# Channel attention on one core: the last loads, the packing of the last block and the re-read ring are rearranged

## The chip, the cores and the metric

The kernel runs on one core of one Trainium2 chip. Its time is the device time of one execution in microseconds (us); the figure for the kernel before is the median of three runs, 727.28 us (724.67 to 727.91). Stage times are read from one profiled execution of it.

## The reference

The input x has 384 x 384 pixels of 384 channels in bf16; w1 is 384 x 96 and w2 96 x 384.

```python
xf = x.reshape(B, H * W, C)
gap = jnp.mean(xf, 1)
gmp = jnp.amax(xf, 1)
h_a = gap @ w1
h_a = h_a * (h_a > 0)
h_m = gmp @ w1
h_m = h_m * (h_m > 0)
scale = _sigmoid(h_a @ w2 + h_m @ w2)
return x * scale[:, None, None, :]
```

Each channel's mean and maximum over all pixels go through a small two-layer gate, and every pixel is multiplied by the 384 gate values. All of x has to be read before the first product can be made.

## The kernel before, in words

The pixels are cut into 1152 "rows". One row is 128 pixels, one to a partition, with 384 channels each: 96 KB. The input and the output are 1152 rows each, and the core's SBUF holds only a part of them, so the kernel has two phases.

**First phase.** SP issues the loads (L396) in the order of the list `steps`. For each load TensorE adds the rows up with a vector of ones (L290; for the last four loads L306, straight into `gsum_ps`), and VectorE takes the maximum of the rows into the accumulator `acc` of 11 rows (L360). `acc` is worked on in two halves by turns. FEWER says at which load, counted from the end, it is folded from 11 rows to 8.

Some rows remain on the chip for the second phase, so they need not be read again. Eight blocks of 32 rows are packed into the space of 24 each: ScalarE tests that the high bytes are in a small range (`test`, L319 and L320), TensorE makes 16-bit words of them in PSUM (`pack`, L340, into `words_ps`, with weights of which two lie in `held`), and ScalarE takes the result (L346 and L347). Ten rows go to PSUM early (`kept_ps`, `kept_b`). 64 rows "stay" where transient rows lay before. Eight "late" rows are loaded into `d_places[0]` and transposed by TensorE into the PSUM bank of the words (`turn_over`, L366), eight "kept" rows into `d_places[1]`, and five "held" rows into `held`. `held` is also where the tests write their bytes and where two of the packing weights lie, so the held load, which is the last of all, can only be issued when the last test and the last words are done.

All other rows pass through and are read once more in the second phase.

**The gap.** After the last load SP issues, in this order: eight rows for the place that the last packing frees (L425), w1 (L426), w2 (L427), eight rows for `d_places[0]` as soon as the late rows have been transposed out of it (L439), and the eleven rows of the accumulator's own pixels in four pieces, as folding frees them (L437). TensorE's program in this stretch is: the turn of the sums (L301), the sums of the last four loads with the transposes of the late rows after the first of them (L306, L366, L306), then the first layer of the gate for the mean, which needs w1 (L430), then the transposes of the folded maximum (L450), the first layer for the maximum (L454) and the second layer (L456). An engine works off its program in order, so L450 can't start before L430 has. ScalarE makes the sigmoid (L457) and the second phase begins.

**Second phase.** VectorE multiplies rows by the gate (L462) and ScalarE's queue issues their stores (L471, L477, L512): first what stayed, then the ring. PLACES lists the places of the ring: a place is read again (L547, on SP) when the product of the rows that lay there has been stored, and its turn comes in order. TURNS says in which turn a packed block is unpacked by VectorE and ScalarE (L490, L495, L509); two finished blocks let the ring grow from 72 rows to 96 and to 120.

The order on every engine is the order in which the code records it (`manual_schedule`). DMAs get one of eight completion semaphores in turn, and a DMA waits until the one eight before it has landed.

These are the lists that set the end of the first phase. LAST_BLOCK's two loads, PASSING's eight, STAYING's ten and LAST_HELD's four are the last 24 loads; PACK_LAST puts the two halves of the last block's packing ahead of the 19th and the 11th load from the end.

```python
FEWER = {16: 8}
LAST_BLOCK = (10, 22)
PACK_LAST = {19: 0, 11: 1}
PASSING = ((0, 20), (20, 16), (36, 17), (53, 11), (0, 11), (11, 8), (19, 8), (27, 12))
REFILLS = (5, 6)
STAYING = ((39, (4, 8, 5, 8)), (0, (8, 4, 9, 8, 6, 4)))
LAST_HELD = ((8,), (4, 4), (5,))
```

Of the kernel before, what the change touches and what calls it, by code (L numbers as in the profile page):

```python
# [19 lines left out]
E4 = mybir.dt.float8e4  # L20
E3 = mybir.dt.float8e3
# [10 lines left out]
G = 8  # L32
PACKED = 8
# [14 lines left out]
LATE_ROWS = 8  # L48
BANK_ROWS = 2
RING_BYTES = 128  # L50
HELD_ROWS = 5
A = 11

FEWER = {16: 8}

ACC_PIECES = ((6, 11), (0, 6))

# [8 lines left out]
PACK_BEHIND = (0, 2, 1, 1, 0, 0, 1)  # L66

LAST_BLOCK = (10, 22)
PACK_LAST = {19: 0, 11: 1}
PASSING = ((0, 20), (20, 16), (36, 17), (53, 11), (0, 11), (11, 8), (19, 8), (27, 12))  # L70

REFILLS = (5, 6)
STAYING = ((39, (4, 8, 5, 8)), (0, (8, 4, 9, 8, 6, 4)))
LAST_HELD = ((8,), (4, 4), (5,))


PLACES = (
    ((0, 18), (18, 18), (36, 18), (54, 18)) * 3 + ((0, 24), (24, 24), (48, 24), (72, 24))
    + ((0, 30), (30, 30), (60, 30), (90, 30)) * 3 + ((0, 30), (30, 30), (60, 30), (90, 12))
)  # L80
FIRST_READ = (6, 12)
# [24 lines left out]
def kernel(  # L106
# [7 lines left out]
    nc = tc.nc  # L114
    P = nc.NUM_PARTITIONS
    B_, H, W_, C = x.shape
# [19 lines left out]
    at = 0  # L136

    def take(n):
        nonlocal at
        at += n  # L140
        return at - n, n

    for_psum = PSUM_ROWS + BANK_ROWS
    first_block = take(for_psum + A)
    packed_block = take(GP * PACKED)
    late_block, kept_block, held_block = (take(sum(pieces)) for pieces in LAST_HELD)
    stay = take(STAY_ROWS)
    refills = [take(PASSING[k][1]) for k in REFILLS]
    passing_at, n_pass = at, TOT - at
    between = [[take(n) for _, n in group] for group in BETWEEN]  # L150
    passing = [refills[REFILLS.index(k)] if k in REFILLS else take(n) for k, (_, n) in enumerate(PASSING)]
    assert at == TOT and sum(n for _, n in PLACES) == n_pass and held_block[1] == HELD_ROWS
    assert late_block[1] == LATE_ROWS and kept_block[1] == G and [n for _, n in refills] == [LATE_ROWS, G]
    assert sum(sum(p) for _, p in STAYING) == STAY_ROWS
    at = passing_at
    again = [take(n) for _, n in PLACES]
# [3 lines left out]
    ones_bf = small[:, 0:1]  # L160
# [6 lines left out]
    total = small[:, 1:2]  # L167
# [10 lines left out]
    acc = consts.tile([P, A, C], BF16)  # L178
# [3 lines left out]
    rows = nc.alloc_sbuf_tensor_at("rows", [P, HELD_ROWS + BODY_ROWS, C], BF16, offset=RING_BYTES).ap()  # L182
    held, body = rows[:, 0:HELD_ROWS, :], rows[:, HELD_ROWS:HELD_ROWS + BODY_ROWS, :]
# [3 lines left out]
    d_places = fourth[0:2]  # L187
# [12 lines left out]
    late = words_ps[:, 0:LATE_ROWS, :]  # L200
# [30 lines left out]
    weights = []  # L231
# [9 lines left out]
    def load(block, buf, pieces, lo=0):  # L241
        j = 0
        for m in pieces:
            steps.append(("load", block, buf[:, j:j + m, :], lo + j, lo + j + m))
            j += m
# [17 lines left out]
                steps.append(("pack", i, 1))  # L263
    i = PACKED - 1
    load(packed_block, body[:, D_AT[i]:, :], LAST_BLOCK, FOURTH_AT[i])
    steps += [("test", i, 0), ("test", i, 1), ("test", i, 2), ("judge",)]
    for k, b in enumerate(passing):
        fill(b, PASSING[k][0])
    for lo, pieces in STAYING:
        load(stay, body[:, lo:, :], pieces, lo)  # L270
    for block, buf, pieces in zip((late_block, kept_block, held_block), (*d_places, held), LAST_HELD):
        load(block, buf, pieces)

    loads = [st for st in steps if st[0] == "load"]
    tail_rows = sum(st[4] - st[3] for st in loads[len(loads) - SUM_TAIL:])
# [1 line left out]
    def high(rows, dt):  # L277
        return rows.rearrange("p n c -> p (n c)").bitcast(dt)[:, 1::2]
# [4 lines left out]
    def part(i, r):  # L283
        return homes[i][:, r * G:(r + 1) * G, :] if r < 3 else fourth[i]
# [39 lines left out]
    def test(i, what):  # L324

        if what == 2:
            test_one(high(part(i, 3), I8), 5 * i + 4)
            return
        n = G * C // 2
        a_b = homes[i][:, 0:2 * G, :].rearrange("p (r n) c -> p r (n c)", r=2).bitcast(I8)  # L330
        test_one(a_b[:, :, 2 * n * what + 1:2 * n * (what + 1):2], 5 * i + 2 * what)
        test_one(high(part(i, 2), I8)[:, n * what:n * (what + 1)], 5 * i + 2 * what + 1)

    def pack(i, half):
        n = G * C // 2
        span = slice(half * n, (half + 1) * n)
        for c in range(0, n, BANK):
            for r in range(4):
                for k, dt in enumerate((E4, E3)):
                    nc.tensor.matmul(  # L340
                        words[:, c:c + BANK], lhsT=weights[2 * r + k],
                        rhs=high(part(i, r), dt)[:, half * n + c:half * n + c + BANK],
                        start=(r == 0 and k == 0), stop=(r == 3 and k == 1),
                    )
        for r in (0, 1):
            nc.scalar.copy(out=high(part(i, r), U8)[:, span], in_=low(part(i, r + 2), U8)[:, span])  # L346
        nc.scalar.activation(  # L347
            out=part(i, 2).rearrange("p n c -> p (n c)").bitcast(U16)[:, span], in_=words,
            func=ACT.Copy, bias=32767.5,
        )  # L350

    def judge():
# [3 lines left out]
    def judged():  # L356
        nc.tensor.matmul(bad_ps, lhsT=total, rhs=ones_bf, start=True, stop=True)

    def maximum(out_, in0, in1):
        nc.vector.tensor_tensor(out=out_, in0=in0, in1=in1, op=ALU.max)  # L360
# [1 line left out]
    def turn_over(out_, rows):  # L362

        for r in range(LATE_ROWS):
            for q in range(CQ):
                nc.tensor.transpose(  # L366
                    out=out_[:, r, q * P:(q + 1) * P], in_=rows[:, r, q * P:(q + 1) * P], identity=ident_bf
                )
# [11 lines left out]
    for st in steps:  # L380
        if st[0] == "test":
            test(*st[1:])
        elif st[0] == "pack":
            pack(*st[1:])
        elif st[0] == "judge":
            judge()
        if st[0] != "load":
            continue
        _, block, rows, lo, hi = st
        m = hi - lo  # L390
        if len(loads) - nth in PACK_LAST:
            half = PACK_LAST[len(loads) - nth]
            if half == 1:
                judged()
            pack(PACKED - 1, half)
        nc.sync.dma_start(out=rows, in_=rows_of(xr, block)[:, lo:hi, :])  # L396
        if nth < len(loads) - SUM_TAIL:
            sums(rows, m, done, TOT - tail_rows)
# [12 lines left out]
        while j < m:  # L411
            c, e = halves[turn % len(halves)]
            turn += 1
            e = min(e, c + m - j)
            maximum(acc[:, c:e, :], acc[:, c:e, :], rows[:, j:j + e - c, :])
            j += e - c
        if block == late_block:
            turn_over(late, rows)
        elif block == first_block:
            nc.vector.tensor_copy(out=kept_ps.bitcast(U32), in_=rows[:, 0:PSUM_ROWS, :].bitcast(U32))  # L420
            nc.vector.tensor_copy(out=kept_b.bitcast(U32), in_=rows[:, PSUM_ROWS:for_psum, :].bitcast(U32))
        nth += 1


    nc.sync.dma_start(out=fourth[PACKED - 1], in_=rows_of(xr, refills[1]))  # L425
    nc.sync.dma_start(out=w1_sb, in_=w1.rearrange("(q p) m -> p q m", p=P))  # L426
    nc.sync.dma_start(out=w2_sb, in_=w2)  # L427
    nc.scalar.mul(out=gT[:, :, 0], in_=gsum_ps, mul=1.0 / HW)
# [1 line left out]
        nc.tensor.matmul(hTa_ps, lhsT=w1_sb[:, q, :], rhs=gT[:, q, 0:1], start=(q == 0), stop=(q == CQ - 1))  # L430
    nc.scalar.activation(out=hid_a, in_=hTa_ps, func=ACT.Relu)

    def acc_rows(ap, lo, hi):
        return rows_of(ap, first_block)[:, for_psum + lo:for_psum + hi, :]

    def load_acc(lo, hi):
        nc.sync.dma_start(out=acc[:, lo:hi, :], in_=acc_rows(xr, lo, hi))  # L437

    nc.sync.dma_start(out=d_places[0], in_=rows_of(xr, refills[0]))  # L439
    load_acc(folds[-1], A)  # L440
    half = folds[-1] // 2
    fold(half)
    load_acc(half, 2 * half)
# [111 lines left out]

    put_stay(*OPENING)
    put_acc()
    put(held_block, held, (HELD_ROWS,))
    put(kept_block, d_places[1], (G,))
    put(refills[0], d_places[0], (LATE_ROWS,))  # L560
    put_stay(*FIRST_PLACE)
# [75 lines left out]
```

## Time and profile before

| | |
|---|---|
| median of three runs | 727.28 us (724.67 to 727.91) |
| the profiled execution, its own time | 724.8 us |
| its span in the profile | 723.0 us |
| busy: VectorE, ScalarE, TensorE matmuls | 574.5, 358.8, 191.6 us |
| read from HBM, written to it | 192.14 MB, 113.25 MB |
| mean rate of the DMA engines | 423 GB/s |
| granted TensorE clock, mean | 0.627 |
| end of the last maximum of the first phase | 272.1 us |
| first product | 276.75 us |

The profile's page cuts the span into 40 slices of 18.1 us. Its DMA row gives the busy share of the 16 DMA engines in tenths and its GB/s row what they moved. The answer by windows gives the same for stretches that one names. The timeline has one line per group of instructions: start, duration, engine, line, operation, and in square brackets how long the engine was idle before it and who ended that. SPq and ACTq are the queues of SyncE and ScalarE on which DMAs are issued; the duration on such a line is that of the issue alone. A list of DMA issues gives KB and the time from issue to landing. The chain of waits is followed back from the last instruction of a stretch to what released it.

### The profile page before, as it was taken

What the parts mean: (1) busy time and instruction counts of PE and PEld (TensorE: products, weight loads), DVE (VectorE), ACT (ScalarE), POOL (GpSimd) and SP (SyncE); (2) the same over time, 40 slices, a digit from 0 to 9 for tenths busy, and PEclk for the clock granted to TensorE, in tenths of its full rate; (3) what the DMA queues carried; (4) which work ended last, traced back from release to release, by engine and by line L of the source; (5) the groups of instructions that cost most, each with busy time, mean ns of one, the idle gap of its engine ahead of it and who ended that gap; (6) DMA issues with size and microseconds to landing.
All of it is one profiled execution on the core that took longest, in us unless ns stands there. A gap on an engine that the chain in (4) does not pass through costs nothing.

```text
span 723.0 us, 4062 instructions
## 1 busy us (share of the span) xinstructions
PE 191.6 (26%) x1405; PEld 75.5 (10%) x1405; DVE 574.5 (79%) x463; ACT 358.8 (50%) x284; POOL 0.7 (0%) x6
## 2 busy tenths in 40 slices
PE   5667575966776681000000000000000000001000
PEld 2222222321322240000000000000000000001000
DVE  5699899999999998887876659837899999837300
ACT  6967969694989940350540635404544745000000
POOL 0000000000000000000000000000000000000000
PEclk9887987895978776555555555555555555555555
DMA  9999999999999999999999999999999999999997
GB/s 381 435 434 433 421 432 429 428 427 430 428 421 428 414 382 347 406 424 429 430 429 431 433 434 435 429 437 433 430 428 432 433 438 428 428 432 433 450 424 334
DMA packets 22422, 305.66 MB, mean 423 GB/s; under 512 B 2848, under 2 KB 3072, under 8 KB 8704
## 3 DMA queue, kind: packets, MB, share of 16 engines
q1 hardware_dynamic: 14336, 192.14, 62.6%
q10 hardware_dynamic: 8064, 113.25, 36.7%
q8 instruction: 11, 0.18, 0.1%
q14 instruction: 11, 0.09, 0.0%
HBM read 192.14 MB, written 113.25 MB: 422 GB/s over the span
## 4 chain that ended last, share of the span: by engine, by line
DMA 53%; DVE 25%; issue 6%; ACT 5%; PE 4%; SPq 0%; DVEq 0%; ACTq 0%
DMA rows<-in_x_dram 41%; DVE rows L462 14%; DMA out_dram<-rows 11%; DVE acc L360 5%; DVE rows L490 3%; ACT rows L319 3%; PE bank_a L290 2%; PE words_ps L340 2%; ACT rows L320 1%; DVE acc L495 1%; DVE acc L490 1%; ACT rows L346 1%; ACT rows L347 0%; DVE acc L462 0%; SPq L396 0%
## 5 line engine op out<-in xcount | busy, mean ns | idle before, releaser
L462 DVE TENSOR_TENSOR rows<-rows,scale_bc 128x11520 bf16<-128x11520 bf16 (+8 forms) x60 | 231.6, 3897 | 79.0 <-DMA rows<-in_x_dram 66.7
L360 DVE TENSOR_TENSOR acc<-acc,rows 128x2304 bf16<-128x2304 bf16 (+4 forms) x234 | 245.8, 1127 | 14.0 <-DMA rows<-in_x_dram 13.5
L509 ACT COPY rows<-rows 128x1536 uint8<-128x1536 uint8 x32 | 47.2, 1476 | 155.7 <-DVE rows L462 126.4
L290 PE MATMUL bank_a<-rows,small 128*1 128x512 bf16 (+2 forms) x891 | 92.4, 466 | 80.4 <-DMA rows<-in_x_dram 80.3
L366 PE MATMUL words_ps<-ident_bf,acc 128*128 128x128 bf16 x24 | 2.7, 313 | 384.1 <-DVE acc L592 384.1
L319 ACT ACTIVATE rows<-rows,tests 128x3072 uint8<-128x3072 int8 (+1 forms) x40 | 93.6, 2341 | 21.9 <-DMA rows<-in_x_dram 21.1
L509 ACT COPY rows<-acc 128x1536 uint8<-128x1536 uint8 x48 | 69.1, 1473 | 39.1 <-DVE acc L495 38.6
L346 ACT COPY rows<-rows 128x1536 uint8<-128x1536 uint8 x32 | 45.5, 1471 | 23.9 <-PE words_ps L340 23.9
L320 ACT ACTIVATE rows<-rows,tests 128x1536 uint16<-128x1536 uint16 (+1 forms) x40 | 52.8, 1319 | 1.3
L290 PEld LDWEIGHTS <-small 128*1 128x1 bf16 x891 | 30.2, 96 | 139.4 <-issue 117.9
L340 PE MATMUL words_ps<-rows,scale_bc 128*128 128x512 fp8e4 x144 | 43.7, 417 | 3.8 <-ACT rows L347 3.8
L366 PEld LDWEIGHTS <-acc 128*128 128x128 bf16 x24 | 2.5, 149 | 384.5 <-DVE acc L592 384.5
L340 PE MATMUL words_ps<-rows 128*128 128x512 fp8e3 x144 | 39.6, 385 | 0.0
L490 DVE TENSOR_SCALAR rows<-rows 128x1536 uint16<-128x1536 uint16 x64 | 35.8, 560 | 2.2
L340 PE MATMUL words_ps<-rows,w_sb 128*128 128x512 fp8e3 x96 | 30.2, 398 | 0.0
L509 ACT COPY acc<-rows 128x1536 uint8<-128x1536 uint8 x16 | 23.5, 1466 | 0.0
L347 ACT ACTIVATE rows<-words_ps 128x1536 uint16<-128x1536 f32 x16 | 23.0, 1439 | 0.0
L340 PEld LDWEIGHTS <-scale_bc 128*128 128x128 bf16 x144 | 13.7, 103 | 27.1 <-issue 14.2
L340 PEld LDWEIGHTS <-rows 128*128 128x128 bf16 x144 | 14.4, 100 | 18.3 <-issue 2.4
L495 DVE SCALAR_TENSOR_TENSOR rows<-rows 128x768 uint32<-128x768 uint32 x16 | 15.3, 959 | 0.6
L495 DVE SCALAR_TENSOR_TENSOR acc<-acc,rows 128x768 uint32<-128x768 uint32 x16 | 15.3, 958 | 0.6
L340 PEld LDWEIGHTS <-w_sb 128*128 128x128 bf16 x96 | 10.0, 104 | 13.5 <-issue 3.8
(61 smaller groups left out, 61.3 us busy)
## 6 DMA issues: line engine op xcount, KB each, us to landing
rows<-in_x_dram SPq DMA_DIRECT2D x16, 2880.0 KB, 22.6
out_dram<-rows ACTq DMA_DIRECT2D x15, 2880.0 KB, 25.0
out_dram<-rows ACTq DMA_DIRECT2D x13, 1728.0 KB, 15.1
rows<-in_x_dram SPq DMA_DIRECT2D x11, 1728.0 KB, 15.9
rows<-in_x_dram SPq DMA_DIRECT2D x7, 2304.0 KB, 18.6
rows<-in_x_dram SPq DMA_DIRECT2D x4, 3072.0 KB, 35.2
out_dram<-rows ACTq DMA_DIRECT2D x4, 3072.0 KB, 23.7
out_dram<-rows ACTq DMA_DIRECT2D x5, 2304.0 KB, 17.9
```

Source lines behind the costliest of these rows:

```text
L290: nc.tensor.matmul(sum_ps[q * QP:q * QP + 1, 0:g * P], lhsT=ones_bf[:, 0:1], rhs=rows[:, k:k + g, q * P:(q + 1) * P], start=(done + k == 0 ...
L319: nc.scalar.activation(out=out_, in_=rows, func=ACT.Square, bias=test_bias, scale=TEST_SCALE)
L320: nc.scalar.activation(out=pairs, in_=pairs, func=ACT.Square, bias=minus, accum_out=tests[:, k:k + 1],)
L340: nc.tensor.matmul(words[:, c:c + BANK], lhsT=weights[2 * r + k], rhs=high(part(i, r), dt)[:, half * n + c:half * n + c + BANK], start=(r ...
L346: nc.scalar.copy(out=high(part(i, r), U8)[:, span], in_=low(part(i, r + 2), U8)[:, span])
L347: nc.scalar.activation(out=part(i, 2).rearrange("p n c -> p (n c)").bitcast(U16)[:, span], in_=words, func=ACT.Copy, bias=32767.5,)
L360: nc.vector.tensor_tensor(out=out_, in0=in0, in1=in1, op=ALU.max)
L366: nc.tensor.transpose(out=out_[:, r, q * P:(q + 1) * P], in_=rows[:, r, q * P:(q + 1) * P], identity=ident_bf)
L462: nc.vector.tensor_tensor(out=dst, in0=src, in1=scale_bc.unsqueeze(1).to_broadcast([P, n, C]), op=ALU.mult)
L490: nc.vector.tensor_scalar(out=u16(dst), in0=u16(src), scalar1=s1, scalar2=s2, op0=op0, op1=op1)
L495: nc.vector.scalar_tensor_tensor(out=u32(v), in0=u32(v), scalar=0x3F3F3F3F, in1=u32(m), op0=ALU.bitwise_xor, op1=ALU.bitwise_xor)
L509: nc.scalar.copy(out=dst, in_=src)
```

## The change

The held rows are no longer read last. They become an eighth passing load, ahead of the twelve rows, and five rows are read into `held` in the gap instead (`refills[2]`), first of all the gap's DMAs. The late rows are loaded seven loads sooner, before the second part of the staying rows, and are transposed behind the third load from the end. The last block's words are made by TensorE in six thirds of eight matmuls, ahead of the loads 20, 19, 18, 13, 12 and 11 from the end; ScalarE's tests of that block stand around the taking of the first half, and the judging (with TensorE's `bad_ps`) comes later. The load of the accumulator's rows 8 to 10 is issued before w1 and w2. Folding to 8 rows comes before the 14th load from the end's maxima. The fourth round of the ring has five places (18, 18, 18, 18, 24 rows) in place of four of 24.

```diff
-FEWER = {16: 8}
+FEWER = {14: 8}
...
-PACK_LAST = {19: 0, 11: 1}
-PASSING = ((0, 20), (20, 16), (36, 17), (53, 11), (0, 11), (11, 8), (19, 8), (27, 12))
-
-REFILLS = (5, 6)
-STAYING = ((39, (4, 8, 5, 8)), (0, (8, 4, 9, 8, 6, 4)))
-LAST_HELD = ((8,), (4, 4), (5,))
+LAST_WORDS = (20, 19, 18, 13, 12, 11)
+PASSING = ((0, 20), (20, 16), (36, 17), (53, 11), (0, 11), (11, 8), (19, 8), (27, 5), (32, 12))
+
+REFILLS = (5, 6, 7)
+STAYING = ((44, (8, 4, 8)), (0, (8, 4, 9, 8, 6, 5, 4)))
+LAST_HELD = (4, 4)
+
+TURN_BEHIND = 3
...
-    ((0, 18), (18, 18), (36, 18), (54, 18)) * 3 + ((0, 24), (24, 24), (48, 24), (72, 24))
+    ((0, 18), (18, 18), (36, 18), (54, 18)) * 3 + ((0, 18), (18, 18), (36, 18), (54, 18), (72, 24))
...
-    for lo, pieces in STAYING:
-        load(stay, body[:, lo:, :], pieces, lo)
-    for block, buf, pieces in zip((late_block, kept_block, held_block), (*d_places, held), LAST_HELD):
-        load(block, buf, pieces)
+    load(stay, body[:, STAYING[0][0]:, :], STAYING[0][1], STAYING[0][0])
+    load(late_block, d_places[0], (LATE_ROWS,))
+    load(stay, body[:, STAYING[1][0]:, :], STAYING[1][1], STAYING[1][0])
+    load(kept_block, d_places[1], LAST_HELD)
...
-        if len(loads) - nth in PACK_LAST:
-            half = PACK_LAST[len(loads) - nth]
-            if half == 1:
-                judged()
-            pack(PACKED - 1, half)
+        if len(loads) - nth in LAST_WORDS:
+            half, third = divmod(LAST_WORDS.index(len(loads) - nth), 3)
+            make_words(PACKED - 1, half, third)
+            if third == 2:
+                if half == 0:
+                    test(PACKED - 1, 0)
+                take_words(PACKED - 1, half)
+                if half == 0:
+                    test(PACKED - 1, 1)
+                    test(PACKED - 1, 2)
+                else:
+                    judge()
...
-        if block == late_block:
-            turn_over(late, rows)
-        elif block == first_block:
+        if len(loads) - nth == TURN_BEHIND:
+            turn_over(late, d_places[0])
+        if block == first_block:
...
+    nc.sync.dma_start(out=held, in_=rows_of(xr, refills[2]))
     nc.sync.dma_start(out=fourth[PACKED - 1], in_=rows_of(xr, refills[1]))
+    nc.tensor.matmul(bad_ps, lhsT=total, rhs=ones_bf, start=True, stop=True)
...
+    load_acc(folds[-1], A)
     nc.sync.dma_start(out=w1_sb, in_=w1.rearrange("(q p) m -> p q m", p=P))
     nc.sync.dma_start(out=w2_sb, in_=w2)
...
     nc.sync.dma_start(out=d_places[0], in_=rows_of(xr, refills[0]))
-    load_acc(folds[-1], A)
...
-    put(held_block, held, (HELD_ROWS,))
+    put(refills[2], held, (HELD_ROWS,))
```

`make_words` holds the loop of `pack` over one third of the words, `take_words` its two ScalarE copies and the activation. In the lists of instructions the change leaves the number of loads of the first phase at 57. VectorE has one maximum fewer in the first phase and one product more in the second, SP one read of five rows more in the gap and one of the ring more (four of 24 rows become one of 24 and four of 18).

More of the change, by code (lines that the diff above doesn't have):

```diff
@@ L145 @@
     packed_block = take(GP * PACKED)
-    late_block, kept_block, held_block = (take(sum(pieces)) for pieces in LAST_HELD)
+    late_block, kept_block = take(LATE_ROWS), take(sum(LAST_HELD))
     stay = take(STAY_ROWS)
@@ L151 @@
     passing = [refills[REFILLS.index(k)] if k in REFILLS else take(n) for k, (_, n) in enumerate(PASSING)]
-    assert at == TOT and sum(n for _, n in PLACES) == n_pass and held_block[1] == HELD_ROWS
-    assert late_block[1] == LATE_ROWS and kept_block[1] == G and [n for _, n in refills] == [LATE_ROWS, G]
+    assert at == TOT and sum(n for _, n in PLACES) == n_pass
+    assert late_block[1] == LATE_ROWS and kept_block[1] == G and [n for _, n in refills] == [LATE_ROWS, G, HELD_ROWS]
     assert sum(sum(p) for _, p in STAYING) == STAY_ROWS
@@ L265 @@
     load(packed_block, body[:, D_AT[i]:, :], LAST_BLOCK, FOURTH_AT[i])
-    steps += [("test", i, 0), ("test", i, 1), ("test", i, 2), ("judge",)]
     for k, b in enumerate(passing):
         fill(b, PASSING[k][0])
-    for lo, pieces in STAYING:
-        load(stay, body[:, lo:, :], pieces, lo)
-    for block, buf, pieces in zip((late_block, kept_block, held_block), (*d_places, held), LAST_HELD):
-        load(block, buf, pieces)
+    load(stay, body[:, STAYING[0][0]:, :], STAYING[0][1], STAYING[0][0])
+    load(late_block, d_places[0], (LATE_ROWS,))
+    load(stay, body[:, STAYING[1][0]:, :], STAYING[1][1], STAYING[1][0])
+    load(kept_block, d_places[1], LAST_HELD)
     loads = [st for st in steps if st[0] == "load"]
@@ L332, in test, with make_words, take_words @@
         test_one(high(part(i, 2), I8)[:, n * what:n * (what + 1)], 5 * i + 2 * what + 1)
-    def pack(i, half):
+    def make_words(i, half, third):
+        n = G * C // 2
+        c = third * BANK
+        for r in range(4):
+            for k, dt in enumerate((E4, E3)):
+                nc.tensor.matmul(
+                    words[:, c:c + BANK], lhsT=weights[2 * r + k],
+                    rhs=high(part(i, r), dt)[:, half * n + c:half * n + c + BANK],
+                    start=(r == 0 and k == 0), stop=(r == 3 and k == 1),
+                )
+    def take_words(i, half):
         n = G * C // 2
         span = slice(half * n, (half + 1) * n)
[L337 to L344, printed above, removed]
         for r in (0, 1):
@@ L350, in pack @@
         )
+    def pack(i, half):
+        for third in range(3):
+            make_words(i, half, third)
+        take_words(i, half)
     def judge():
@@ L354, in judge @@
         nc.scalar.copy(out=total, in_=test_sum)
-    def judged():
-        nc.tensor.matmul(bad_ps, lhsT=total, rhs=ones_bf, start=True, stop=True)
     def maximum(out_, in0, in1):
@@ L384 @@
             pack(*st[1:])
-        elif st[0] == "judge":
-            judge()
         if st[0] != "load":
@@ L422, with acc_rows, load_acc @@
         nth += 1
+    nc.sync.dma_start(out=held, in_=rows_of(xr, refills[2]))
     nc.sync.dma_start(out=fourth[PACKED - 1], in_=rows_of(xr, refills[1]))
+    nc.tensor.matmul(bad_ps, lhsT=total, rhs=ones_bf, start=True, stop=True)
+    def acc_rows(ap, lo, hi):
+        return rows_of(ap, first_block)[:, for_psum + lo:for_psum + hi, :]
+    def load_acc(lo, hi):
+        nc.sync.dma_start(out=acc[:, lo:hi, :], in_=acc_rows(xr, lo, hi))
+    load_acc(folds[-1], A)
     nc.sync.dma_start(out=w1_sb, in_=w1.rearrange("(q p) m -> p q m", p=P))
@@ L431 @@
     nc.scalar.activation(out=hid_a, in_=hTa_ps, func=ACT.Relu)
[L433 to L437, printed above, removed]
     nc.sync.dma_start(out=d_places[0], in_=rows_of(xr, refills[0]))
-    load_acc(folds[-1], A)
     half = folds[-1] // 2
```

## The prediction

> **What bounds the kernel now.** I read the page's slices first.
>
> ```profile
> DMA  9999999999999999999999999999999999999997
> GB/s 381 435 434 433 421 432 429 428 427 430 428 421 428 414 382 347 406 424 429 430 429 431 433 434 435 429 437 433 430 428 432 433 438 428 428 432 433 450 424 334
> ```
>
> The DMA engines are busy from end to end. Only the first, the last and slices 15 to 17 (about 253 to 307 us) move clearly less: the gap between the phases. So I asked for windows across it (columns: window, length, busy and count of PE, PEld, DVE, ACT and POOL, clock, DMA share, GB/s).
>
> ```profile
> 254.00:264.00 10.00, 7.71 (x32) 3.00 (x29) 9.89 (x13) 3.63 (x4) 0.00 (x0) 0.61 1.02 413
> 264.00:268.00 4.00, 3.50 (x45) 1.30 (x43) 3.87 (x6) 3.97 (x5) 0.00 (x0) 1.00 0.94 352
> 268.00:272.00 4.00, 3.87 (x95) 3.79 (x95) 4.00 (x6) 0.48 (x2) 0.00 (x0) 1.00 0.74 264
> 272.00:276.00 4.00, 1.47 (x15) 0.76 (x11) 2.77 (x7) 0.34 (x2) 0.00 (x0) 0.92 0.95 313
> 276.00:279.00 3.00, 0.14 (x1) 0.00 (x0) 2.25 (x3) 0.49 (x1) 0.00 (x0) 0.50 0.76 291
> 279.00:282.00 3.00, 0.00 (x0) 0.00 (x0) 3.00 (x4) 0.00 (x0) 0.00 (x0) 0.50 0.94 373
> ```
>
> Against the 413 GB/s ahead of it, the gap leaves (61 + 149 + 100) x 4 + (122 + 40) x 3 = 1726 us x GB/s = 1.73 MB unused, 17.6 rows of 96 KB or 4.2 us. That is all that can be won there. What fixes its length is the chain of waits.
>
> ```profile
> 254.36 12.96 DMA rows<-in_x_dram
> ...
> 270.90 1.23 DVE acc L360 x2
> 272.13 0.02 issue
> 272.15 0.97 DVE acc L360
> 273.14 0.57 DVE acc L360
> 273.74 0.37 DVE acc L360
> 274.11 0.05 issue
> 274.15 0.28 PE bank_a L450 x2
> ```
>
> The late rows' landing (254.36 + 12.96 = 267.3), VectorE's maxima of the last 21 rows, the three folds, the transposes, then the gate; the first product starts at 276.75, its store is issued at 277.54. The gate hangs on the maxima, not on DMAs. Lastly TensorE's timeline and the list of DMA issues, asked at the issue times of the gap (264.79 held rows, 266.34 L425, 269.01 w1).
>
> ```profile
> 269.66 1.50 PE L366 MATMUL words_ps<-ident_bf,rows 128*128 128x128 bf16 x24
> 271.00 1.12 PE L306 MATMUL bank_b<-small,rows 128*128 128x1 bf16 x39
> 272.72 0.29 PE L430 MATMUL bank_b<-small,w_sb 128*96 128x1 bf16 x3 [0.60 <-DMA w_sb<-in_w_dram]
> 274.15 0.28 PE L450 MATMUL bank_a<-ident_bf,acc 128*128 128x128 bf16 x2 [1.14 <-DVE acc L360]
> ```
> ```profile
> rows<-in_x_dram SPq DMA_DIRECT2D x1, 480.0 KB, 5.6
> ...
> rows<-in_x_dram SPq DMA_DIRECT2D x1, 768.0 KB, 6.1
> ...
> w_sb<-in_w_dram SPq DMA_DIRECT2D x1, 72.0 KB, 3.7
> ```
>
> Landings, issue plus time: held 264.79 + 5.6 = 270.4, L425 272.4, w1 272.7. They come in the order of their issue, though w1 is small. L430 starts as w1 lands and has 1.14 us to spare before L450. That margin carries this prediction.
>
> **The change part by part.**
>
> *The first phase's end.* Still 1152 rows are read, so the last row lands when it did: from 267.3 to 270.4 came 4 + 4 + 5 rows, 0.237 us a row. I keep 270.4; bounds are 40 rows at the 0.231 us a row of the 425 GB/s earlier (0.25 us sooner) and the same later.
>
> *VectorE's tail.* A maximum of 128x1536 takes 952 ns and the next starts 0.87 after it; of 768 and 384, 0.47 and 0.27. After the change the last seven loads are 9, 8, 6, 5, 4, 4, 4 rows. The nine land 31 rows before the end, at 270.4 - 31 x 0.237 = 263.1; nine maxima of four rows, one of two and two of one follow: 9 x 0.87 + 0.47 + 2 x 0.27 = 8.8, so the folds start at 272.0. Before: 272.15. Taking the held rows off the end wins nothing there, because VectorE is 1 to 2 us behind the landings in both.
>
> *ScalarE and TensorE.* The tests and takes are the same instructions in another order. From the timeline a half's tests of three parts take 7.2 us, the last test 4.6, a take 4.2, the judging 0.6. The first half's last third follows the sums of the 19th load (landed 241.2): 241.2 + 1.5 + 3.4 = 246.1, take to 250.3, tests to 262.1. The second half's thirds start behind the 14th load's sums at 252.5; they run 7.5 us in one piece now (257.15 to 264.7), with sums between them 261.4. Take to 266.3, judged 266.9, the sums turned by about 268.5: w1 is issued near 268.8, as now (269.01). Nothing waits for this yet.
>
> The granted clock in that run is 0.50 for the first third (3.4 us for eight matmuls) and 0.88 to 1.00 for the rest. [...] The row bounds this as well: three cold thirds are 10.2 us, the end 264.0, the take 268.2, w1's issue 270.6; with 3.7 us to land, 274.3. By either the next term decides, so the sum is unchanged, but the cover is then used up.
>
> *The gap's DMAs.* Held rows (5), L425's eight and the accumulator's three now stand ahead of w1 on SP's queue; before only L425's eight did. All are issued before the last row lands, since their waits (late words, tests, takes) end by 266.3. So w1 lands after 16 rows instead of 8: 270.4 + 16 x 0.237 + 0.25 (w1 behind L425 now) = 274.45. The nearest slower row is L425 itself, 2.02 us for eight: 274.7. L430 starts 0.04 later, takes 0.29, and L450 can't start before: 274.8, instead of 274.15. **So the gate comes 0.6 us later**; bounds 0 (w1 as now) and 0.9.
>
> *The five rows more* cost 5 x 0.237 = 1.2 us of DMA and fit in the 4.2 unused: 24 rows and the weights are through by 276.5 or so, the accumulator's last eight by 278.6 (now 279.2). The transposes of the late rows (1.5 us) now run before the last landing, so `d_places[0]` is loaded without the wait that ended at 271.2. That fills the DMAs but brings no product forward. If it were not hidden it would cost 1.2 us.
>
> *The second phase.* Until 290 us stores follow the products: the first four land 2.4, 2.4, 2.6 and 2.8 us after issue for 3, 4, 5 and 6 rows, that is 1.5 to 1.7 us beyond their transfer, unqueued. What the gate loses the whole phase loses, since behind it the DMA share is 1.00 to 1.01 and the rows to read (774) and to write (1152) are the same.
>
> *The fifth place.* 72 rows go in pieces of 18 instead of 24. The window 320 to 400 (18s) moved 431 GB/s, 424 to 456 (24s) 434: 14.2 MB at the one instead of the other is 0.2 us. Reads are issued a turn sooner; with a share of 1.01 there is no idle time to win. Should it lift the 18s' whole stretch of 111 us from 431 to 434, -0.8. I take +0.1, nearest to the first.
>
> **Sum**: 0 + 0.6 + 0.1 = +0.7 us. On the profiled execution: 724.8 + 0.7 = 725.5. That execution lies 2.5 us below the median of the three; on the median 727.28 + 0.7 = **728.0**.
>
> **Rivals.**
>
> 1. *w1 isn't held up.* If w1 lands near 272.7 + 1.4 or sooner, L450 stays at 274.15 and only the ring's term is left: 727.3. Against: the landings above in order of issue. For: my margin is 0.6. [...]
> 2. *Faster.* The DMAs' unused 4.2 us less the 1.2 of the new rows could be won if the second phase were bound by them and not by the gate: -3.0, and with the ring's -0.8 -3.8 at most. A part of it, -1.2, gives 726.1. For: DMA 53% of the chain. Against: the stores after the gate are unqueued.
> 3. *Slower: the last words come late.* L425, w1, w2 and `d_places[0]` stand on SP behind the second take, the turning of the sums on ScalarE behind it too. From a take that ends at 268.2 on, every us later is one on w1, L430, L450 and the gate. Two us give 730; 0.5% (3.6 us) needs the take at 271.2 or later, 5 us after my estimate. For: cold thirds use up the cover. Against: no wait of that size in the sum.
>
> **Chances.** About 0.5% (3.6 us) is what a measurement of this kernel can tell from no change. Forecast (slip of 0.3 to 1.2) 0.52; rival 1 0.20; rival 2 0.13, of which 0.06 beyond 0.5%; rival 3 0.15, of which 0.07. So faster 0.06, same 0.87, slower 0.07. The range takes in a median at the fast end of the runs (724.67, less some of rival 2) and rival 3 at two to three us: 724.0 to 730.5.
>
> **What will show it.** L430's wait (L451 after) ended by w1 at about 274.5, L450's successor (L464) starting right behind it and no longer ended by VectorE, the first product at 277.4; the last maxima ending at 272; GB/s above 380 from 264 to 276. I am wrong if w1 lands by 273.8, if the first product moves by over 1.5 us, if loads of the first phase land late because thirds hold up the sums, or if the ring's stretch from 400 to 480 loses its share of 1.01.

## The result and the profile after

The changed kernel is slower: 732.76 us median of six runs (730.58 to 734.61) against 726.17 us (724.67 to 727.92) for six runs of the kernel before, the earlier three among them. The ratio is 1.0088, with a 95% interval of 1.0061 to 1.0115: some 6.4 us, or 4.4 to 8.4. I had forecast 728.0, no difference that can be told. The profiled execution of the changed kernel took 733.83 us (span 732.0) beside 724.8 us (span 723.0) before, so the two traces lie 9 us apart, more than the 6.4 us of the runs.

First the rates in the page's 40 slices, after the change.

```profile
DMA  9999999999999999999999999999999999999997
GB/s 384 425 439 425 432 435 427 427 429 428 425 427 422 415 361 368 401 424 434 425 433 429 429 433 426 431 421 401 434 404 436 383 422 404 426 438 428 443 431 324
```

The gap (slices 15 to 17) looks much as before. What is new are the slices 401, 404, 383 and 404 late in the second phase, between about 494 and 622 us, where before had 428 to 438 in slices 25 to 36. The DMA row above them shows nothing: it is 9 in each of these.

The windows across the gap, after:

```profile
264.00:268.00 4.00, 1.68 (x14) 0.55 (x13) 4.00 (x7) 0.53 (x3) 0.00 (x0) 0.75 1.03 405
268.00:272.00 4.00, 4.00 (x52) 3.99 (x53) 4.00 (x6) 0.52 (x2) 0.00 (x0) 0.50 0.93 357
272.00:276.00 4.00, 2.60 (x42) 2.24 (x40) 2.55 (x6) 0.34 (x2) 0.00 (x0) 0.50 0.65 218
276.00:279.00 3.00, 0.84 (x4) 0.32 (x3) 1.58 (x4) 0.49 (x1) 0.00 (x0) 0.50 0.82 309
279.00:282.00 3.00, 0.00 (x0) 0.00 (x0) 3.00 (x4) 0.00 (x0) 0.00 (x0) 0.50 0.84 320
```

The last column falls later and lower than before (218 from 272 to 276, where before had 313). Multiplied out, with 411 GB/s from 254 to 264, the 28 us from 254 to 282 moved 9.92 MB; the same windows before moved 9.84 MB. The gap has 0.49 MB more to read after the change and moved 0.08 MB more.

The chain of waits across the gap, after:

```profile
269.28 5.44 DMA w_sb<-in_w_dram
...
274.76 0.40 PE bank_b L451 x3
275.16 0.25 PE bank_a L464 x2
...
277.70 0.78 DVE rows L476 x2
```

The gate now hangs on the landing of w1 and no longer on VectorE's folds. TensorE's timeline shows the same from the engine's side:

```profile
270.25 2.72 PE L372 MATMUL words_ps<-ident_bf,rows 128*128 128x128 bf16 x24
...
274.76 0.40 PE L451 MATMUL bank_b<-small,w_sb 128*96 128x1 bf16 x3 [1.07 <-DMA w_sb<-in_w_dram]
275.02 0.37 PE L464 MATMUL bank_a<-ident_bf,acc 128*128 128x128 bf16 x2
```

L451 (L430 before) waits 1.07 us for w1, and L464 (L450 before) stands right behind it, as the prediction said: it starts at 275.02, though the folds ended at 274.16. The first line the prediction did not say: the transposes took 2.72 us instead of 1.50, at a granted clock of 0.50 instead of 1.00.

Now the ring. Windows of before:

```profile
400.00:480.00 80.00, 0.00 (x0) 0.00 (x0) 58.95 (x35) 33.16 (x24) 0.00 (x0) 0.50 1.01 431
480.00:640.00 160.00, 0.00 (x0) 0.00 (x0) 137.03 (x85) 69.16 (x48) 0.00 (x0) 0.50 1.01 433
```

and of after:

```profile
400.00:480.00 80.00, 0.00 (x0) 0.00 (x0) 56.69 (x36) 34.37 (x24) 0.00 (x0) 0.50 1.01 429
480.00:640.00 160.00, 0.00 (x0) 0.00 (x0) 139.11 (x84) 69.15 (x48) 0.00 (x0) 0.50 1.00 415
```

From 480 to 640 us 18 GB/s are missing at an unchanged DMA share: 18 x 160 = 2.88 MB, 6.7 us at 430 GB/s. That is most of the 9 us between the two traces.

What happens there begins a little earlier. The lists of stores issued between 455 and 500 us (KB each, us from issue to landing), before:

```profile
out_dram<-rows ACTq DMA_DIRECT2D x1, 3072.0 KB, 25.7
out_dram<-rows ACTq DMA_DIRECT2D x1, 2304.0 KB, 18.5
```

and after:

```profile
out_dram<-rows ACTq DMA_DIRECT2D x1, 3072.0 KB, 23.7
...
out_dram<-rows ACTq DMA_DIRECT2D x1, 2304.0 KB, 28.1
```

2304 KB are the 24 rows of the last place of the ring's fourth round, 3072 KB the 32 rows that `f3` stores. Before, the trace has the 24 rows issued at 461.1 and landed at 479.5, with the 32 rows behind them at 468.0. After, the 32 rows go first, at 463.8, and the 24 rows follow at 468.6 and land at 496.7. The next two reads (rows 60 to 119 of the ring) need the place of those 24 rows: they were issued at 479.6 and 480.0 before, at 496.8 and 497.2 after, 17 us later.

The reason stands in the two lists. A place is one turn. With five places in the fourth round the place of 24 rows moves from turn 15 to turn 16 (counted from 0), but `f3` stays in `TURNS[15]`: its product and store, behind the 24 rows before, now stand ahead of them.

Last, how the engines can be busy and slow. The DMA queues from 500 to 506 us, after (q1 carries the loads, q10 the stores):

```profile
DMA packets 98, 2.26 MB, mean 376 GB/s; under 512 B 0, under 2 KB 0, under 8 KB 0
...
q1 hardware_dynamic: 93, 2.14, 102.3%
```

The reads alone fill all 16 engines, and yet they move 376 GB/s. 102.3% of 16 x 6 us over 93 packets is 1.06 us each, where the median of a packet of this size (23,040 bytes, 30 rows of one partition) is 0.855 us in the same trace. In the same six us of before, reads (52.7%) and stores (48.2%) share the engines, at 434 GB/s. Stores can be the slow side too: from 570 to 576 us, after, they have 82.9% of the engines and the reads 16.9%, at 369 GB/s (434 before). Yet reads alone aren't slow as such, for the first phase only reads, most of it in packets of other sizes (3,072 to 39,168 bytes), and moves 415 to 439 GB/s in slices 2 to 14 above.

### The profile page after: what moved, and what is told of

The parts are those of the page before. It is cut to its first block, busy times and chain, and to the rows that moved or that the text cites. A ratio compares the mean times of both kernels' runs of the same rounds, so it can differ in the third digit from the quotient of the medians.

```text
span 732.0 us, 4052 instructions
## 1 busy us (share of the span) xinstructions
PE 194.9 (27%) x1396; PEld 76.9 (11%) x1396; DVE 574.4 (78%) x463; ACT 358.9 (49%) x284; POOL 0.7 (0%) x6
## 4 chain that ended last, share of the span: by engine, by line
DMA 53%; DVE 31%; issue 6%; ACT 3%; PE 1%; SPq 0%; DVEq 0%; ACTq 0%
DMA rows<-in_x_dram 35%; DMA out_dram<-rows 17%; DVE rows L476 13%; DVE acc L366 12%; DVE rows L504 3%; ACT rows L523 2%; DVE acc L509 1%; DMA w_sb<-in_w_dram 1%; DVE acc L504 1%; ACT acc L523 1%; SPq L407 0%; DVE acc L476 0%; PE bank_b L302 0%; DVE rows L509 0%; PE bank_a L291 0%
## 5 line engine op out<-in xcount | busy, mean ns | idle before, releaser
L476 DVE TENSOR_TENSOR rows<-rows,scale_bc 128x6912 bf16<-128x6912 bf16 (+8 forms) x61 | 231.6, 3836 | 84.6 <-DMA rows<-in_x_dram 80.9
```

Source lines behind the costliest of these rows:

```text
L476: nc.vector.tensor_tensor(out=dst, in0=src, in1=scale_bc.unsqueeze(1).to_broadcast([P, n, C]), op=ALU.mult)
```

## The experiments

The working theory (A) was the order just shown: late reads, then reads and stores by turns, each alone at a time, with slow packets. Theory B: what the gap loses makes the ring late and slow. Theory C: five places are slower by themselves. Ratios are against the kernel before, run beside each; its median was 726.95 us beside e1 to e4, 726.73 beside e5 to e8, 725.34 beside e9 to e11 and 725.28 beside e12. Differences in us below come from the ratios, which are not those of the medians. In order of what they settle:

| kernel | median us | ratio (95% interval) | first read of the ring | GB/s 480 to 640 |
|---|---|---|---|---|
| the change | 732.76 | 1.0088 (1.0061 to 1.0115) | 293.2 | 415 |
| e1 the change with the old ring | 728.91 | 1.0024 (1.0003 to 1.0045) | 293.2 | 432 |
| e2 before with the fifth place | 730.62 | 1.0043 (1.0022 to 1.0064) | 291.1 | 419 |
| e3 the change, f3 a turn later | 729.0 | 1.0029 (1.0010 to 1.0047) | 293.2 | 433 |
| e5 before with fifth place, f3 later | 726.62 | 1.0005 (0.9986 to 1.0025) | 290.9 | 433 |
| e6 before, f2 and f3 a turn sooner | 728.55 | 1.0026 (1.0007 to 1.0044) | 291.3 | 424 |
| e4 old ring, w1 first | 728.48 | 1.0034 (1.0014 to 1.0053) | 294.0 | 432 |
| e7 e3 with nine matmuls more | 726.94 | 1.0015 (0.9997 to 1.0034) | 291.9 | 432 |
| e8 e3, rows 8 to 10 behind w1 | 729.26 | 1.0028 (1.0012 to 1.0045) | 293.2 | 433 |
| e9 before with nine matmuls fewer | 726.87 | 1.0005 (0.9990 to 1.0021) | 292.6 | 432 |
| e10 the change with nine matmuls more | 731.35 | 1.0069 (1.0042 to 1.0097) | 292.0 | 421 |
| e11 e7 without the held refill | 729.27 | 1.0040 (1.0024 to 1.0056) | 291.7 | 433 |
| e12 before with five rows more | 728.1 | 1.0029 (1.0013 to 1.0046) | 291.7 | 432 |

The first read before is issued at 290.86, and its 480 to 640 moves 433.

**Which part costs.** e1 puts the old places back into the changed kernel, e2 puts the new ones into the kernel before:

```diff
-    ((0, 18), (18, 18), (36, 18), (54, 18)) * 3 + ((0, 24), (24, 24), (48, 24), (72, 24))
+    ((0, 18), (18, 18), (36, 18), (54, 18)) * 3 + ((0, 18), (18, 18), (36, 18), (54, 18), (72, 24))
```

> The changed kernel with the ring of before (fourth round of four places of 24 rows); the gap stays as changed. Theory A, the loss is in the ring: the last 24-row place is stored behind f3's 32 rows, the reads of the rows from 60 on come late, reads and stores then run by turns and packets of 23040 B take 1.1 to 2.3 us instead of 0.855. Then the 5 to 6 us that the changed kernel loses from 400 us on go, and 1 to 2.5 us of the gap remain: 727 to 729 us, a DMA rate of about 433 GB/s from 480 to 640 us. Theory B, the loss is a late consequence of the gap (stores begin 1 to 2 us later, so that reads and stores meet out of step): about 732 us, 412 to 418 GB/s there.

> The kernel before with nothing but the fifth place in the fourth round. Theory A: the gap is as before (first product 276.75 us), and 4 to 6 us are lost from 400 us on: 730 to 732 us. Theory B: no more than 0.5 us from before, 726 to 727 us.

The ring alone gives +0.43%, 3.1 us, less than the 4 to 6 expected; everything else alone +0.24%, 1.7 us. The sum, 1.0067, lies in the interval of the whole change, near its lower end. The window from 480 to 640 of e2 shows the ring's loss without any change in the gap:

```profile
480.00:640.00 160.00, 0.00 (x0) 0.00 (x0) 135.80 (x84) 69.15 (x48) 0.00 (x0) 0.50 1.00 419
```

Theory B falls as the main cause, and keeps the smaller part.

**The order, or the five places?** e3 puts an empty turn ahead of `f3` in the changed kernel; e5 does the same in e2.

```diff
-    ... "3a", "3b", "f3", "", "1a", "1b",
+    ... "3a", "3b", "", "f3", "", "1a", "1b",
```

> The changed kernel with an empty turn ahead of f3, so that f3 and all behind it keep their distance from the places: the 24-row place is stored ahead of f3's 32 rows again, as in the kernel before. Theory A in its narrow form (the order of these two stores): 727 to 729 us, the read of the rows from 60 on issued by 485 us instead of 496.8. Theory A in its wide form (five places as such, since the last of them is stored one turn later): still 731 to 734 us. Theory B: 732 us too.

> The kernel before, with the fifth place of the ring and an empty turn ahead of f3; nothing else of the change. Theory A (the fifth place costs time because f3's store of 32 rows then goes ahead of the store of the 24-row place, so that the reads of the rows from 60 on come some 15 us late, and reads and stores run by turns): the 24 rows are stored before the 32, those reads are issued at about 480 instead of 494, 480 to 640 runs at 430 GB/s or more (fifth place alone: 419), and the time is that of before, 726.0 to 727.5 us. Theory C (a ring of five places is slower by itself, by the size of its transfers): 729.5 to 731, with 480 to 640 at 420 GB/s or less.

In both the 24 rows are stored ahead of the 32 again (463.9 and 470.4 in e3; 461.4 and 468.0 in e5), the first of the two reads comes at 481.2 and 479.9, and 433 GB/s are back. e5 can't be told from the kernel before in time (-1.0 to +1.8 us), with its fifth place: five places as such cost nothing that these runs can tell (theory C falls), and win nothing. The empty turn moves f3 and all work behind it, so what is shown is the order of the jobs against the places; that the two stores alone are enough is argued. e6 makes the bad order without a fifth place, by taking the empty turn between 2a and 2b out of the kernel before.

```diff
-    ... "f0", "", "2a", "", "2b", "f2", "3a", "3b", "f3", ...
+    ... "f0", "", "2a", "2b", "f2", "3a", "3b", "f3", ...
```

> The kernel before with its ring of four places, and the empty turn between 2a and 2b taken out, so that f2, f3 and the later work come a turn sooner: f3's store of 32 rows then goes ahead of the last store of 24 rows without any fifth place. Theory A (that order is what costs): the reads of the rows from 60 on are issued 10 us or more later than before's 479.6, 480 to 640 runs at 415 to 422 GB/s instead of 433, and the time is 729.5 to 731. Theory C (five places are slower by themselves): 726 to 727.5.

Its 32 rows go at 458.6, its 24 rows at 463.4, the reads at 492.5, and the rate falls:

```profile
480.00:640.00 160.00, 0.00 (x0) 0.00 (x0) 139.09 (x84) 69.14 (x48) 0.00 (x0) 0.50 1.00 424
```

So the order costs time where there are four places too, though e6 moves f2 and the later jobs along with f3. Direction and place are as expected, the size is not: +0.26%, 1.9 us, where 3 to 4 were expected, and 424 GB/s where at most 422 were. Theory A stands; how much such a disorder costs isn't a fixed price.

**The gap's part.** e4 (with the old ring) issues w1 and w2 ahead of the held rows' refill; e8 (with the empty turn) moves the load of the accumulator's rows 8 to 10 behind `d_places[0]` again.

```diff
# e4
+    nc.sync.dma_start(out=w1_sb, in_=w1.rearrange("(q p) m -> p q m", p=P))
+    nc.sync.dma_start(out=w2_sb, in_=w2)
     nc.sync.dma_start(out=held, in_=rows_of(xr, refills[2]))
# e8
-    load_acc(folds[-1], A)
     nc.sync.dma_start(out=w1_sb, in_=w1.rearrange("(q p) m -> p q m", p=P))
...
     nc.sync.dma_start(out=d_places[0], in_=rows_of(xr, refills[0]))
+    load_acc(folds[-1], A)
```

> The changed kernel with the ring of before and with w1 and w2 issued ahead of the five held rows' refill. My reading of the gap: w1 landed 274.7 us behind 16 rows and held the transposes of the maximum; issued first it lands by 272.9, the transposes wait for VectorE again (about 274.3) and the first product comes at 276.8 to 277.0 instead of 277.7, 0.7 to 0.9 us below the kernel with the ring of before alone. But SP then holds the refills until the sums are turned (269.3), so the DMA engines idle 2 us more. If the gate sets the start of the second phase, 0.5 to 1 us faster than the kernel with the old ring alone; if the DMAs do, 1 us slower.

> The changed kernel with the empty turn ahead of f3, and with the load of the accumulator's rows 8 to 10 moved back behind the refill of the eight rows, as in before: w1 is then queued behind 13 rows instead of 16. If the wait for w1 is what the gap costs: w1 lands at about 274.0 instead of 274.7, the first product begins at about 277.0 instead of 277.7, and the time falls by 0.5 to 0.7 us from 729.0. Rival (the gap is bound by what its DMAs have to move, and any order gives the same): the first product comes sooner but the first read of the ring does not move by over 0.3 us, and the time is 728.7 to 729.3.

Both bring w1 sooner (landed at 271.0 and 274.0 instead of 274.7) and with it the first store (277.7 and 277.5 instead of 278.5). Both give it back: the accumulator's rows 4 to 7 land at 279.7 and 279.2 instead of 278.4, VectorE waits for them with the product of the accumulator's first five rows, whose store is issued at 280.9 and 280.5 (280.4 in the change), and the first read of the ring comes no sooner than 293.2. The rival of e8 was right: there the first product begins at 276.69, 0.86 us sooner than in e3, and neither the first read nor the time moves. e4's first read comes at 293.96, 0.8 us later than e1's, and its time can't be told from e1's (1.0034 beside 1.0024). Both kernels also have the cost that follows, so they don't show what the gate is worth without it.

Then a cost that no theory had at first. In the trace of after one packet of the instruction queue falls among the first stores (queues from 278 to 282 us):

```profile
q8 instruction: 1, 0.02, 2.3%
```

0.02 MB are 16,384 bytes; 2.3% of 16 x 4 us is 1.5 us of one DMA engine. The pages of before and after show eleven of them each; before, the last fell at 274.6, ahead of the first store. TensorE has 1396 matmuls and as many weight loads, 2792 instructions, or 254 for each of the eleven, so I take it, as an estimate from these counts, for TensorE's stream. The change leaves TensorE 18 instructions fewer up to the gap; if the fetches keep step with the count, the last one comes later. The list of stores issued from 278 to 283 us, after, ends with the first two:

```profile
out_dram<-rows ACTq DMA_DIRECT2D x1, 384.0 KB, 4.3
out_dram<-rows ACTq DMA_DIRECT2D x1, 288.0 KB, 2.2
```

The first (288 KB) lands 2.2 us after issue, the second to the fifth 4.3 to 4.6, where before had 2.4 for the first and 2.4 to 3.0 for the second to the fifth. I take it that one engine had fallen behind and each of these stores waited for its part; that was not shown, since the trace does not tell the 16 engines apart. The other traces agree on the time: where the fetch falls at 278.9 to 280.5 (the change, e1, e3, e9) the second store lands 4.3 to 4.6 us after issue, where it falls by 275 (before, e2, e5, e6, e7, e10, e11) 2.4 to 2.8; e12 has 3.3 with an early fetch, and in e4 and e8 the fetch comes at 281.8 and 283.1, behind the issue of the first stores. e7 makes up the count with nine small matmuls ahead of the first load, in e3; e10 does so in the whole change; e9 takes nine matmuls out of the kernel before.

```diff
# e7, e10
+    for _ in range(9):
+        nc.tensor.matmul(bad_ps, lhsT=ones_bf, rhs=ones_bf, start=True, stop=True)
     done = turn = nth = 0
# e9
-            sums(rows, m, done, TOT - tail_rows)
+            sums(rows, m - 12 if m == 45 else m, done, TOT - tail_rows)
```

> The changed kernel with the empty turn ahead of f3, and with nine small matmuls ahead of the first read's sums, so that TensorE's count of instructions up to the gap is that of before (18 more than in the change). They use no result of the kernel and are overwritten. Theory A with the fetch as a part of the gap's cost: the fetch of instructions for TensorE falls at 274 to 276 as in before, not at 280.3 among the first stores; the second store lands at about 282 instead of 283.8, the first read of the ring is issued about a microsecond earlier than 293.2, and the time is 1.0 to 1.4 us below that of the kernel with the empty turn alone (729.0), 727.6 to 728.0. Rival: the fetch is a bystander, the DMAs are full in any case; the second store stays at 283.5 or later, and the time at 728.5 to 729.5.

> The whole change, with nine small matmuls ahead of the first read's sums and nothing else, so that the fetch falls where it fell in before. If the two causes add: the stretch from 480 to 640 stays at 414 to 420 GB/s (the ring's part is untouched), the first read of the ring is issued at about 291.9, and the time is 1.0 to 2.0 us below the change's 732.8, 730.8 to 731.8. Rival (they do not add; the late first reads change the ring's order too): the time falls by less than 0.5 us or by more than 3.

> The kernel before, leaving out the sums of 12 rows in one read of 45 rows (nine matmuls, so those rows are missing from the mean): TensorE then has 18 instructions fewer up to the gap, the count of the changed kernel; nothing else of the change. If the place of the fetch of instructions for TensorE is what costs in the gap: the fetch moves from 274.6 to 279 or later, among the first stores; the stores behind it land 1.3 us or more later after their issue than in before, the first read of the ring is issued at about 292.0 to 292.4 instead of 290.9, and the time is 1.0 to 1.5 us above before, 727.7 to 728.3. Rival (the nine matmuls of the experiment before this helped in some other way, or its time was chance): the first read stays at 290.9 and the time at 726.2 to 727.2.

The fetch moves about as expected (273.5 in e7, 274.0 in e10, 278.9 in e9), and the first read of the ring with it. SP issues it at 291.87 in e7, 1.3 us sooner than in e3 (293.21), at 291.99 in e10, 1.2 us sooner than in the change, and at 292.59 in e9, 1.7 us later than before (290.86), by nine matmuls that compute nothing needed or leave out nothing that anyone waits for. In e9, 0.3 of the 1.7 us are there in the first product already (277.02), so the fetch is worth 1.2 us or more at the first read. The times follow less clearly: e7 is 0.14% below e3, e10 0.19% below the change, e9 0.05% above before with an interval from -0.10 to +0.21%, and its 726.87 us lie in the rival's range, so e9's time tells nothing; e7's 726.94 lie below the 727.6 expected. All three have the expected sign and none stands clear of the other by its interval alone: 0.4 to 1.4 us by these values, and none shown. e10's 480 to 640 runs at 421 GB/s, just above the 420 expected.

With the fetch out of the way the first read is late by about what the first product is late: 1.0 and 1.0 us in e7, 1.1 and 0.9 in e10. So in these traces 0.95 of the change's 2.3 us at the first read came with the gate and 1.2 or more with the fetch.

**The five rows.** e11 leaves the refill of `held` out of e7. e12 adds a second read of the five held rows to the kernel before, behind all other loads of the gap.

```diff
# e11
-    nc.sync.dma_start(out=held, in_=rows_of(xr, refills[2]))
# e12
     load_acc(0, 1)
+    nc.sync.dma_start(out=held, in_=rows_of(xr, held_block))
```

> The kernel with the empty turn ahead of f3 and the nine matmuls (726.9), leaving out the refill of the five held rows, so that five stored rows hold other data. w1 is then queued behind 11 rows instead of 16, and 5 rows (0.49 MB) fewer are read. If the five rows in the gap are what is left of the change's cost: w1 lands at 273.5 or sooner, the first product begins at about 276.7 and the first read of the ring at about 290.9 as in before, and the time is 0.6 to 1.2 us below 726.9, 725.7 to 726.3. Rival (as the prediction had it, the five rows find room that was empty): the first product comes sooner, and the time stays at 726.6 to 727.3.

> The kernel before, with a second read of the five held rows (0.49 MB) at the end of the gap, behind the last load of the accumulator, so that w1 and all the other loads of the gap are issued as before and only the bytes grow. If five more rows in the gap cost their bytes (0.49 MB at 430 GB/s, 1.1 us), since the transfers have no room that they do not use later: the load lands by about 281, the first read of the ring is issued 0.8 to 1.2 us later than 290.9, and the time is 0.7 to 1.3 us above before. Rival, as the prediction had it (the five rows go into room that was empty): the first read is issued within 0.3 us of 290.9 and the time is within 0.4 us of before.

e12 came out as the bytes would have it in the gap: the first read moves by 0.86 us, to 291.72. But its five rows are the gap's last load, not the first as in the change. Its time is 2.1 us above before, more than the 0.7 to 1.3 expected; in its trace 400 to 480 runs at 419 GB/s instead of 431. That is a second effect, of the ring again: e4 (421), e1 (422), e8 (424) and e9 (427 GB/s) lost something there too, while e5 (431), e7 and e10 (430) did not, though the first read of e7 and e10 is as late as that of e12. Why isn't settled; all four kernels with the old ring and a first read 0.8 us late or more are among the losers.

e11 missed both of its ranges. w1 landed at 273.4, as expected, but the folds ended at 274.7 (274.1 in before, 274.8 in e7) and the first product came at 277.45, not 276.7; and the time went up instead of down, to 1.0040. At the end of its profile a last few packets still fall behind 724 us (share 0.01), though less is left from 720 to 724 than in e7 (share 0.13 against 0.30), as five rows less would give. What holds these packets up I did not find, so e11's time neither supports nor refutes the price of the rows. In the gap it does say something: it differs from e7 in these five rows alone, and its first read comes at 291.65 instead of 291.87, 0.2 us sooner, no more than its first product (0.3 us).

No kernel beat the kernel before; e5, e7 and e9 can't be told from it.

## Why the prediction was wrong

- **The fifth place, +0.1 with bounds from -0.8 to +0.2: this is the step that failed.** It measured +3.1 us (1.6 to 4.7, from e2's interval), against +1.7 (0.2 to 3.3, e1) for all the rest, where the sum had +0.6. I priced the pieces by the GB/s of neighbouring windows and set "reads are issued a turn sooner" at nothing, without laying `PLACES` beside `TURNS`. A fifth place is a fifth turn, and it moved one store behind another one on ScalarE's queue. e3 and e5 show that the order of the jobs against the places, and not the number of places, is the cause; why packets get slow when reads and stores go by turns stays open.
- **The sign that I named to watch was the wrong one.** I looked for a DMA share below 1.01 from 400 to 480. The share stayed at 1.00 to 1.01 while the rate fell to 415 GB/s from 480 to 640. So here the share hardly told 415 GB/s (1.00) from 433 (1.01); the last column did.
- **"They fit in the 4.2 unused": its sign failed, its price isn't settled.** I took an unused rate for room. My sign for it, above 380 GB/s from 264 to 276, failed: 405, then 357, then 218. The idle transfers lie from 270 on (share 0.73 and 0.69 in the 3 us from 270 and from 273, 1.04 in those ahead of them), where SP issues no load between 270.2 and 273.0, and the five rows were asked for ahead of that. The gap moved 0.08 MB more though it had 0.49 MB more to read, so about 0.41 MB, 1.0 us, came later; but the stores that the fetch and the gate hold back are in that sum as well. e12 has 0.86 us for the same bytes at the end of the gap, e7 and e11 only 0.2 us at the place where the change has them.
- **"`d_places[0]` is loaded without the wait that ended at 271.2": failed.** It was issued at 273.0. The transposes began 0.6 us later than before and ran at half clock. The thirds had moved TensorE's work ahead, its busy time from 262 to 266 is 1.59 of 4 us, and the clock fell to 0.50 at 266 and stayed there; that the one follows from the other was not shown. TensorE is busy 4.00 of 4.00 us from 268 to 272 and the next window is still at 0.50; in e8, after the same transposes in 2.72 us, the clock was back (0.95 from 273 to 276), and what brings it back was not shown either. I had weighed that clock for the thirds and not for what comes after them.
- **The fetch of instructions**, 1.2 us or more at the first read and 0.4 to 1.4 us in times that are not clear of noise, was not in the sum at all.
- **The gate, +0.6: right.** w1 landed at 274.72 (forecast 274.45), L464 stood behind L451, and the first product came at 277.70, 0.95 us later than before, just past my bound of 0.9. e7 and e10, without the late fetch, pass that lateness on to the first read of the ring. In e4 and e8, with the fetch among the stores, taking it away brought the first read no sooner. Of the first four stores in before, the part beyond their transfer is 1.4 to 1.7 us, not 1.5 to 1.7 as I wrote; nothing hangs on it.
- **VectorE's tail and the words: right.** The folds began at 272.21 (forecast 272.0; before 272.15), though at 272.7 to 272.9 in e7, e10 and e11. The second take ended at 263.7, sooner than my 266.3, so rival 3 did not happen, and nothing of rival 2 showed.
- **Rival 1 (w1 isn't held up): ruled out.** w1 landed 5.4 us after issue behind 16 rows (274.7), at 274.0 behind 13 in e8, at 273.4 behind 11 in e11, and 2.0 us after issue in e4, with nothing of the refills ahead of it: in order, in each of these runs.

## What to carry to other kernels

Where two written lists meet turn by turn, as places and jobs do here, a change of length in one shifts every later step of the other: write out the order of stores and reads before and after, and follow which read waits for which store. Read rate beside share, since DMA engines that were 100% busy here were 4% slow (415 for 433 GB/s). And idle transfers in a stage are not room for more bytes by themselves: five rows more at the end of the gap put the first read off by 0.86 us, so ask when the idle time comes and what can be issued then.

## What the runs showed of the hardware

- Packets of 23,040 bytes, 0.855 us in the median, took 1.06 us on average from 500 to 506 us while the reads had the engines almost to themselves (102.3%, the stores 4.5%). One direction alone isn't enough for it: the first phase, with reads alone, moves 415 to 439 GB/s in the same run, and the last stores, alone from 700 to 716 us, still move 427 GB/s in the kernel before.
- A fetch of 16 KB of instructions among the stores took one DMA engine 1.5 us, and the second store landed 1.9 us later after its issue (4.3 for 2.4), the next three 1.6 to 1.8 us later (4.4, 4.5 and 4.6 for 2.6, 2.8 and 3.0). Nine matmuls more or fewer, far ahead, decide where it falls (273.5 in e7 for 280.3 in e3, 278.9 in e9 for 274.6 in before).
- TensorE's granted clock did not come back in 4 us of unbroken transposes and sums (busy 4.00 of 4.00 from 268 to 272) behind a stretch of 1.59 us busy in 4; in e8 it was back from 273 on (0.95 from 273 to 276).
